# Two spectral filters mixed by a gate: rows folded four ways, the swapped spectrum made by DMA, products in column chunks

## The chip, the core and the metric

The kernel runs on one core of a Trainium2 chip. TensorE (PE) multiplies matrices into PSUM; ScalarE (ACT) and VectorE (DVE) read PSUM and write SBUF; GpSimd (POOL) takes small copies; transfers are issued by SyncE's queue (SP) and carried by 16 DMA engines. The metric is device time in microseconds (us), the median of the runs.

## The reference

`x` is a real image of 2048 rows and 1024 columns in bfloat16. Two filters A and B have complex weights of 2048 rows and 513 columns each, given as real and imaginary parts. Both filters read the same `x`; `B_x` is not used.

```python
def _A_ref(x, w_r, w_i):
    X = rfft2(x.astype(float32))
    X = X * (w_r + 1j * w_i)
    return irfft2(X, s=(S, D)).astype(bfloat16)

x = A_x
g = sigmoid((x * gate_w).sum(-1, keepdims=True))
a = _A_ref(x, A_w_r, A_w_i)
b = _B_ref(x, B_w_r, B_w_i)
return g * a + (1 - g) * b
```

## The kernel before

The transforms are matrix products. A row number is split as n = 64 n1 + n2 (n1 of 32, n2 of 64), a row frequency as k = k1 + 32 k2. The seven stages are numbered as in the code; a "t" is one of 16 values of the first row frequency, and each t yields two of the 32 values of k1.

- Load (L252 to L266). SP issues constants M in four pieces alternating with four pieces of 1 MB of x, then F2 and CK, then the weights W as 32 transfers of 64 partitions, 4 rows of 513 values each. Real parts lie on partitions 0 to 63, imaginary parts on 64 to 127.
- Stage 1 (L273 to L300). Partition p holds 16 whole rows of x. The column half is folded: DVE makes a reversed copy of the second half (L274), PE multiplies the plain and the reversed half with M (L295), ACT evicts (L299). Between the reversed copies DVE forms the 16 dot products of x with `gate_w` (L278).
- Stage 2 (`stage2`, L306). For one t: 8 matmuls of 512 columns (L314), one ACT eviction (L317), one tiny POOL copy into STAR (L319).
- Stage 4 (`stage4`, L322). For one t, four matmuls of 512 columns make the row spectrum X and four more make the swapped one (real and imaginary parts exchanged between partition halves, from shifted columns of the same matrices, `64 * sw`); L336, evicted by ACT at L339. Then four DVE products of 128x1024 with W (L348), two into R_A, two into R_W. Stage 2 of t+1 stands ahead of stage 4 of t on PE.
- After all products, in this order: the table U5 is loaded over F2 and M (L358); the gate's diagonal (L362), a matmul that spreads it (L366), the sigmoid (L371); the Nyquist column ("star", L376, L384, L386); a POOL copy (L393); a correction of column 0 (L410, L412).
- Stage 5 (L436 to L461): 32 groups g of 16 matmuls of 128 columns (L449), evicted by ACT and DVE in turn (L458). DVE forms the gated row tables (`rbgen`, L429), four small products for each r.
- DI is loaded after the last stage 5 matmul, over dead rows of R_A (L465).
- Stage 6 (`stage6`, L470) is 16 matmuls of 128 for one r with an ACT eviction (L485); stage 7 (`stage7`, L487) is 8 matmuls of 512 (L494), one ACT eviction (L498), two DVE additions (L502) and a store of 256 KB. Stage 6 of r+2 stands ahead of stage 7 of r.

The order on every engine is the order in which `P.add` is called; `Prog` turns the read and write keys into semaphore waits. A wait on DVE is for a count of its finished instructions, so whoever waits for one DVE result waits for all that stand ahead of it:

```python
                elif op.needed:
                    c += 1
                    op.sem, op.count = sem("s_" + e), c
```

Of the kernel before, what the change touches and what calls it, by code (L numbers as in the profile page):

```python
# [4 lines left out]
dt = mybir.dt  # L5
ACT = mybir.ActivationFunctionType
ALU = mybir.AluOpType
# [3 lines left out]
RW = 514  # L11
NROW = 64 * RW
# [9 lines left out]
def make_consts():  # L22

    C = {}
    pi2 = 2 * np.pi
    n1 = np.arange(32)
    M = np.zeros((32, 4, 16, 16, 2, 4))
    for b in range(4):  # L30
        for r in range(16):
            n2 = 16 * b + r
            for t in range(16):
                if t == 0:
                    M[:, b, r, 0, 0, b] = 1.0
                    M[:, b, r, 0, 1, b] = (-1.0) ** n1
                else:
                    ph = pi2 * t * (64 * n1 + n2) / 2048
                    M[:, b, r, t, 0, b] = np.cos(ph)
                    M[:, b, r, t, 1, b] = -np.sin(ph)  # L40
    M = M.reshape(128, 16, 1, 128)
    C["M"] = np.concatenate([M, -M], axis=2).reshape(128, 16 * 256)
    dd = np.arange(512)[:, None]
    ll = np.arange(512)[None, :]
    th = pi2 * ll * (dd + 0.5) / 1024
    cs, sn = np.cos(th), np.sin(th)
    sn[:, 0] = (-1.0) ** np.arange(512)
    F2 = np.stack([cs.reshape(4, 128, 512), sn.reshape(4, 128, 512)])
    C["F2"] = F2.transpose(2, 0, 1, 3).reshape(128, 8 * 512)
# [3 lines left out]
    def four(kind, pm):  # L53
# [11 lines left out]
        return Ac.reshape(128, 128), Bs.reshape(128, 128)  # L65

    blocks = []
    for kind in ("gen", "sp"):
        for pm in range(2):
            for m in four(kind, pm):  # L70
                blocks += [m, m[:, :64]]
# [3 lines left out]
    KIA = np.block([[c, s], [-c, -s]])  # L75
    KIB = np.block([[-s, c], [-s, c]])
    blocks += [KIA, KIB]
# [10 lines left out]
    blocks += [T1, T3, -T3, T3z, -T3z, T2, T4, -T4, T4z, -T4z]  # L88
    blocks += [np.eye(128), np.ones((128, 128))]
    C["CK"] = np.concatenate(blocks, axis=1)  # L90
    row = np.arange(128)
    l2, k1, f = row % 2, (row // 2) % 32, row // 64
# [11 lines left out]
    C["SM"] = SM  # L104
    DI = np.zeros((128, 2, 2, 2, 512))
    d = np.arange(512)[None, :]
    for lb in range(2):
        for h in range(2):
            l0 = 128 * lb + np.arange(128)
            l = l0 + 257 * h  # L110
            if h == 1 and lb == 1:
                l[127] = 256
            l = l[:, None]
            cl = np.where(l == 0, 1.0, 2.0) / D
            a = pi2 * l * (d + 0.5) / 1024
            DI[:, lb, h, 0] = cl * np.cos(a)
            DI[:, lb, h, 1] = -cl * np.sin(a)
# [81 lines left out]
def bass_gated_mix__spectral_gfnet__spectral_gfnet__prompt_kernel(nc, A_x, A_w_r, A_w_i, B_x, B_w_r, B_w_i, gate_w, out):  # L199
# [6 lines left out]
    NK = C["CK"].shape[1]  # L206
    R_A = sb("R_A", NROW)
    R_W = sb("R_W", NROW)
    R_F = sb("R_F", 16384)
    R_M = sb("R_M", 8192)  # L210
    CK = sb("CK", NK)
    RING = sb("RING", 7184)
    RB = sb("RB", 2048)
    DZ = sb("DZ", 2048)
# [4 lines left out]
    ZS = sb("ZS", 16, dt.float32)  # L219
    PS = nc.alloc_psum_tensor("PS", [128, 4096], dt.float32)  # L220

    def sl(t, off, dims, p0=0, np_=128):
        n = t.shape[1]
        return AP(t, p0 * n + off, [[n, np_]] + [list(x) for x in dims])
# [4 lines left out]
    CSO, XAO, XSO = 0, 3 * 1028, 3 * 1028 + 2048  # L229
    FB = {}  # L230
    i = 0
    for kind in range(2):
        for pm in range(2):
            for m in range(2):
                FB[kind, pm, m] = 192 * i
                i += 1
    KIAo, KIBo = 1536, 1664
    TO = [1792 + 128 * j for j in range(10)]
    IDo, ONo = 1792 + 1280, 1792 + 1408
# [4 lines left out]
    xv = x2.rearrange("(p r) d -> p r d", r=16)  # L244
    outv = out2.rearrange("(p r) d -> p r d", r=16)

# [3 lines left out]
    u16 = dt.uint16  # L250
    GWo = 0
    dma("act", sl(RB, GWo, [(1, 1024)]), AP(gate_w.tensor, gate_w.offset, [[0, 128], [1, 1024]]), w=["gw"])  # L252
    dma("act", SM[:], cst_sm.ap(), w=["SM"])
    for c in range(4):
        dma("sp", sl(R_M, c * 1024, [(1, 1024)]).bitcast(u16), cst["M"].ap()[:, c * 1024:(c + 1) * 1024], w=[("M", c)])
        dma("sp", sl(R_A, c * 4096, [(1024, 4), (1, 1024)]), xv[:, 4 * c:4 * c + 4, :], w=[("x", c)])
    dma("sp", sl(R_M, 4096, [(1, 4096)]).bitcast(u16), cst["F2"].ap(), w=["F2"])
    dma("sp", CK[:].bitcast(u16), cst["CK"].ap(), w=["CK"])
    for c in range(4):
        for hi in range(2):  # L260
            a = 4 * c if hi == 0 else 28 - 4 * c
            for f in range(2):
                for ri in range(2):
                    src = wsrc[f, ri].rearrange("(k2 k1) l -> k2 k1 l", k1=32)[:, a:a + 4, :]
                    dst = sl(R_W, (f * 32 + a) * RW, [(RW, 4), (1, 513)], p0=64 * ri, np_=64)
                    dma("sp", dst, src, w=[("W", a // 4, f, ri)])  # L266

    def bank(b):
        return ("ps", b)

    for c in range(4):  # L273
        P.add("dve", lambda e, c=c: e.tensor_copy(  # L274
            sl(RING, (c % 3) * 2048, [(512, 4), (1, 512)]), sl(R_A, 4 * c * 1024 + 1023, [(1024, 4), (-1, 512)])),
            r=[("x", c)], w=[("xr", c % 3)])
        for r in range(4 * c, 4 * c + 4):
            P.add("dve", lambda e, r=r: e.tensor_tensor_reduce(  # L278
                out=sl(RING, 6144, [(1, 1024)]), in0=sl(R_A, r * 1024, [(1, 1024)]), in1=sl(RB, GWo, [(1, 1024)]),
                scale=1.0, scalar=0.0, op0=ALU.mult, op1=ALU.add, accum_out=ZS[:, r:r + 1]),  # L280
                r=[("x", c), "gw"], w=["zjunk"], a=["z"])

        for j in range(4):
            u = (c * 4 + j) % 4
            for q in range(4):
                r = 4 * c + q
                for h in range(2):
                    if h == 0:
                        lh = sl(R_A, r * 1024 + 128 * j, [(1, 128)])
                        rh = sl(R_M, r * 256, [(0, 2), (1, 128)])  # L290
                    else:
                        lh = sl(RING, (c % 3) * 2048 + q * 512 + 128 * j, [(1, 128)])
                        rh = sl(R_M, r * 256, [(1, 256)])
                    o = ps(u * 1024 + q * 256, [(1, 256)])
                    P.add("pe", lambda e, o=o, lh=lh, rh=rh, h=h: e.matmul(o, lh, rh, start=(h == 0), stop=(h == 1)),  # L295
                          r=[("x", c), ("M", c), ("xr", c % 3)], w=[bank(2 * u + q // 2)])
            src = ps(u * 1024, [(128, 2), (1, 128), (256, 4)])
            dst = sl(R_F, j * 4096 + 4 * c, [(2048, 2), (16, 128), (1, 4)])
            P.add("act", lambda e, s=src, d=dst: e.activation(d, s, ACT.Copy),  # L299
                  r=[bank(2 * u), bank(2 * u + 1)], a=["F1"])  # L300


    order = list(range(1, 16)) + [0]
    ALLX = ["zjunk", ("xr", 0), ("xr", 1), ("xr", 2)]

    def stage2(i):  # L306
        t = order[i]
        b0 = 2 * (i % 2)
        for cs in range(2):
            for j in range(4):  # L310
                lh = sl(R_F, (j * 2 + cs) * 2048 + t * 128, [(1, 128)])
                rh = sl(R_M, 4096 + (cs * 4 + j) * 512, [(1, 512)])
                o = ps((b0 + cs) * 512, [(1, 512)])
                P.add("pe", lambda e, o=o, lh=lh, rh=rh, j=j: e.matmul(o, lh, rh, start=(j == 0), stop=(j == 3)),  # L314
                      r=["F1", "F2"], w=[bank(b0 + cs)])
        ro = CSO + (i % 3) * 1028
        P.add("act", lambda e: e.activation(sl(RING, ro, [(513, 2), (1, 512)]), ps(b0 * 512, [(512, 2), (1, 512)]), ACT.Copy),  # L317
              r=[bank(b0), bank(b0 + 1)], w=[("CS", i % 3)] + ALLX)
        P.add("pool", lambda e: e.tensor_copy(STAR[:, t:t + 1], sl(RING, ro + 513, [(1, 1)])),  # L319
              r=[("CS", i % 3)], a=["STAR"])  # L320

    def stage4(i):  # L322
        t = order[i]
        kind = 0 if t else 1
        ro = CSO + (i % 3) * 1028
        k1s = (t, 32 - t) if t else (0, 16)
        for sw in range(2):
            b0 = 4 + 2 * sw
            for pm in range(2):
                for m in range(2):  # L330
                    lh = sl(CK, FB[kind, pm, m] + 64 * sw, [(1, 128)])
                    if m == 0:
                        rh, o = sl(RING, ro, [(1, 512)]), ps((b0 + pm) * 512, [(1, 512)])
                    else:
                        rh, o = sl(RING, ro + 514, [(1, 511)]), ps((b0 + pm) * 512 + 1, [(1, 511)])
# [16 lines left out]
    for i in range(16):  # L352
        if i + 1 < 16:
            stage2(i + 1)
        stage4(i)
# [222 lines left out]
```

## Time and profile before

| | us |
|---|---|
| median of 3 runs | 181.21 (181.05 to 181.98) |
| span of the profiled execution | 179.5 |
| PE busy / weight load busy | 150.9 / 99.0 |
| DVE busy | 120.5 |
| ACT busy | 112.9 |
| POOL busy | 11.5 |
| bytes moved by DMA | 23.35 MB |

The profiled execution's own time is its span; the runs are timed without the profile, and the difference between 181.21 and 179.5 lies around the span. Busy shares are averages over stages with different limits, so the prediction goes by windows of the span and by the chain of work that ended last. A matmul counted as busy may be waiting inside a full pipeline. Line numbers are those of the kernel before.

### The profile page before, as it was taken

Reading aid. Unit: us, or ns where it says so; the run is one execution under the profiler, and the core shown is the slowest. Engines: PE = TensorE matmul, PEld = TensorE weight load, DVE = VectorE, ACT = ScalarE, POOL = GpSimd, SP = SyncE. Lnnn points to the kernel's source line nnn. Section 1 sums busy time; section 2 is a strip of 40 time slices with the busy share of each in tenths; the row PEclk is TensorE's granted clock in tenths of the full one; section 3 lists DMA queues with packets and bytes.
Section 4 is the critical chain, followed back from the end, with each engine's and each line's share of the span. In section 5 each row is a group of like instructions: output and inputs, shape, how many; then the busy total and the mean of one; then the engine's idle time right before and its main releaser. Section 6 shows DMA issues by size and latency. Waiting matters only on the chain.

```text
span 179.5 us, 3207 instructions
## 1 busy us (share of the span) xinstructions
PE 150.9 (84%) x1304; PEld 99.0 (55%) x1304; DVE 120.5 (67%) x233; ACT 112.9 (63%) x120; POOL 11.5 (6%) x22
## 2 busy tenths in 40 slices
PE   0099557999999999998424999999978999999991
PEld 0078445444444444443102999999966666656640
DVE  0199997067877777787974277888852787765463
ACT  2049668588898888888626355466555665565550
POOL 0000000011131131122001000000000000000000
PEclk9999999999999999999975599999999999999999
DMA  5999999999999940003800000000041213322323
GB/s 131 357 417 430 355 194 193 195 192 198 194 195 198 194 93 0 4 0 84 383 0 0 0 4 4 0 4 0 4 164 75 112 63 119 118 79 100 117 111 123
DMA packets 13038, 23.35 MB, mean 130 GB/s; under 512 B 1121, under 2 KB 9313, under 8 KB 12129
## 3 DMA queue, kind: packets, MB, share of 16 engines
q1 hardware_dynamic: 12736, 22.89, 48.4%
q10 hardware_dynamic: 288, 0.26, 0.6%
q8 instruction: 10, 0.16, 0.4%
q14 instruction: 4, 0.02, 0.1%
HBM read 18.96 MB, written 4.19 MB: 129 GB/s over the span
## 4 chain that ended last, share of the span: by engine, by line
PE 71%; DVE 13%; DMA 7%; ACT 5%; issue 2%; DVEq 0%; SPq 0%; ACTq 0%
PE PS L449 18%; PE PS L314 15%; PE PS L494 15%; PE PS L336 13%; DVE RING L278 7%; PE PS L481 6%; DMA R_A<-in_A_x_dram 4%; DMA R_A<-c_DI 3%; ACT R_F L299 2%; DVE DZ L362 1%; DVE RING L274 1%; DVE R_W L348 1%; ACT RING L339 1%; PE PS L366 1%; DVE R_A L348 1%
## 5 line engine op out<-in xcount | busy, mean ns | idle before, releaser
L339 ACT ACTIVATE RING<-PS 128x1024 bf16<-128x1024 f32 x32 | 32.8, 1024 | 3.5
L449 PE MATMUL PS<-CK,R_A 128*128 128x128 bf16 x256 | 32.6, 230 | 0.0
L449 PE MATMUL PS<-CK,R_W 128*128 128x128 bf16 x256 | 32.6, 230 | 0.0
L449 PEld LDWEIGHTS PS<-CK,R_W 128*128 128x128 bf16 x256 | 31.7, 145 | 0.0
L449 PEld LDWEIGHTS PS<-CK,R_A 128*128 128x128 bf16 x256 | 31.6, 145 | 0.0
L314 PE MATMUL PS<-R_M,R_F 128*128 128x512 bf16 x128 | 30.1, 379 | 1.2 <-ACT R_F L299 1.2
L336 PE MATMUL PS<-RING,CK 128*128 128x512 bf16 (+1 forms) x128 | 30.5, 379 | 0.6 <-ACT RING L339 0.5
L502 DVE TENSOR_TENSOR R_A<-R_A,PS 128x512 bf16<-128x512 f32 x32 | 20.6, 683 | 15.4 <-ACT R_A L498 10.2
L494 PE MATMUL PS<-R_A 128*128 128x512 bf16 x128 | 29.9, 379 | 0.5 <-DMA R_A<-c_DI 0.5
L348 DVE TENSOR_TENSOR R_A<-RING,R_W 128x1024 bf16<-128x1024 bf16 x32 | 22.0, 689 | 12.0 <-ACT RING L339 12.0
L295 PE MATMUL PS<-R_M,R_A 128*128 128x256 bf16 x64 | 16.3, 297 | 12.8 <-DVE RING L274 12.8
L485 ACT ACTIVATE R_A<-PS 128x1024 bf16<-128x1024 f32 x16 | 16.3, 1024 | 16.7 <-PE PS L481 16.7
L348 DVE TENSOR_TENSOR R_W<-RING,R_W 128x1024 bf16<-128x1024 bf16 x32 | 22.0, 689 | 6.6 <-ACT RING L339 6.6
L299 ACT ACTIVATE R_F<-PS 128x1024 bf16<-128x1024 f32 x16 | 15.2, 1032 | 12.6 <-PE PS L295 12.6
L314 PEld LDWEIGHTS PS<-R_M,R_F 128*128 128x128 bf16 x128 | 12.4, 98 | 16.4 <-ACT R_F L299 1.5
L336 PEld LDWEIGHTS PS<-RING,CK 128*128 128x128 bf16 x128 | 12.4, 98 | 16.3 <-ACT RING L339 1.6
L278 DVE CUSTOM_DVE_ANT_0 RING<-R_A,RB 128x1024 bf16<-128x1024 bf16 x16 | 19.6, 1223 | 0.4
L317 ACT ACTIVATE RING<-PS 128x1024 bf16<-128x1024 f32 x16 | 16.4, 1028 | 4.9 <-PE PS L314 4.3
L494 PEld LDWEIGHTS PS<-R_A 128*128 128x128 bf16 x128 | 11.9, 98 | 12.5 <-DMA R_A<-c_DI 0.7
L295 PE MATMUL PS<-R_M,RING 128*128 128x256 bf16 x64 | 16.2, 297 | 0.0
L319 POOL COPY STAR<-RING 128x1 bf16<-128x1 bf16 x16 | 10.6, 662 | 73.6 <-ACT RING L317 73.6
L295 PEld LDWEIGHTS PS<-R_M,R_A 128*128 128x128 bf16 x64 | 6.8, 107 | 14.6 <-DMA R_A<-in_A_x_dram 9.0
(48 smaller groups left out, 141.1 us busy)
## 6 DMA issues: line engine op xcount, KB each, us to landing
R_A<-in_A_x_dram SPq DMA_DIRECT2D x4, 1024.0 KB, 10.4
out_dram<-R_A SPq DMA_DIRECT2D x16, 256.0 KB, 2.0
R_W<-in_A_w_r_dram SPq DMA_DIRECT2D x8, 256.5 KB, 12.9
R_W<-in_A_w_i_dram SPq DMA_DIRECT2D x8, 256.5 KB, 13.0
R_W<-in_B_w_r_dram SPq DMA_DIRECT2D x8, 256.5 KB, 13.1
R_W<-in_B_w_i_dram SPq DMA_DIRECT2D x8, 256.5 KB, 13.4
R_M<-c_U SPq DMA_DIRECT2D x1, 2048.0 KB, 7.5
R_M<-c_M SPq DMA_DIRECT2D x4, 256.0 KB, 8.5
```

Of the source, the lines that this page charges most:

```text
L278: P.add("dve", lambda e, r=r: e.tensor_tensor_reduce(out=sl(RING, 6144, [(1, 1024)]), in0=sl(R_A, r * 1024, [(1, 1024)]), in1=sl(RB, GWo, ...
L295: P.add("pe", lambda e, o=o, lh=lh, rh=rh, h=h: e.matmul(o, lh, rh, start=(h == 0), stop=(h == 1)), r=[("x", c), ("M", c), ("xr", c % 3)], ...
L299: P.add("act", lambda e, s=src, d=dst: e.activation(d, s, ACT.Copy), r=[bank(2 * u), bank(2 * u + 1)], a=["F1"])
L314: P.add("pe", lambda e, o=o, lh=lh, rh=rh, j=j: e.matmul(o, lh, rh, start=(j == 0), stop=(j == 3)), r=["F1", "F2"], w=[bank(b0 + cs)])
L317: P.add("act", lambda e: e.activation(sl(RING, ro, [(513, 2), (1, 512)]), ps(b0 * 512, [(512, 2), (1, 512)]), ACT.Copy), r=[bank(b0), bank ...
L336: P.add("pe", lambda e, o=o, lh=lh, rh=rh, m=m: e.matmul(o, lh, rh, start=(m == 0), stop=(m == 1)), r=["CK", ("CS", i % 3)], w=[bank(b0 + ...
L339: P.add("act", lambda e, xo=xo, b0=b0: e.activation(sl(RING, xo, [(1, 1024)]), ps(b0 * 512, [(1, 1024)]), ACT.Copy), r=[bank(b0), bank(b0 ...
L348: P.add("dve", lambda e, d=dst, a=xin, b=win: e.tensor_tensor(out=d, in0=a, in1=b, op=ALU.mult), r=[("X", sw, i % 2)] + wk, a=[("prod", sw ...
L449: P.add("pe", lambda e, o=o, t=t, l0=l0, ab=ab: e.matmul(o, sl(t, l0, [(257, 128)]), sl(CK, KIAo if ab == 0 else KIBo, [(1, 128)]), start= ...
L485: P.add("act", lambda e, s=src, d=dst: e.activation(d, s, ACT.Copy), r=[bank(b0), bank(b0 + 1)], w=[("Y", r)], after=[last5])
L494: P.add("pe", lambda e, o=o, lh=lh, rh=rh, q=q: e.matmul(o, lh, rh, start=(q == 0), stop=(q == 3)), r=[("Y", r), "DI"], w=[bank(b0 + ri)])
L502: P.add("dve", lambda e, od=od, h=h: e.tensor_tensor(out=od, in0=es, in1=ps((b0 + 1) * 512, [(1, 512)]), op=ALU.add if h == 0 else ALU.sub ...
```

## The change

The whole forward part is laid out anew.

- x is folded four ways: partition 2p+h holds half h of 32 rows. It arrives as 16 transfers of 64 alternate partitions with rows of 512 values (1 KB). M arrives in pieces of 128 values (256 bytes) in eight transfers; POOL makes the negated half of M. There are 32 dot products of 512, some of them now among stage 2.
- Stage 2 has matmuls of 256 columns, 32 for a pair of t, and one ACT eviction of 128x2048 for both; stage 4 has 8 matmuls of 512 for the pair, no swapped ones, and one ACT eviction of 128x2048 into XF. There are 8 pairs.
- Real and imaginary parts lie on even and odd partitions (`PERM`). The swapped spectrum is made by four SBUF-to-SBUF transfers for each pair, each of 64 alternate partitions and two rows of 512 values.
- W goes to alternate partitions too. Three of its eight groups are issued before the first swap, the other five each behind the swaps of a pair.
- Products are made for groups of 16 values of k1 rows (`prod_lb0`, columns 0 to 127 of each half row) during stage 4, and for the other columns afterwards in chunks (`prod_lb1`, `prod_last`). A product reads all rows of a chunk at once, up to 128x2048.
- The gate's diagonal is one DVE instruction at pair 4. Star stands ahead of the seventh group of stage 5, column 0 ahead of the eleventh, the POOL copy ahead of the twenty-first. DVE evicts only every second group from the twenty-first on. The row tables are made by four gate products of 128x2048 and eight scalings.
- U5 has its own tile and is loaded behind the swaps; DI is loaded into XF once all readers of the spectrum are done. Stages 6 and 7 keep their matmuls.

In the new kernel all matmuls of the stages carry the line of the helper `mm`, evictions and copies that of `move`, products that of `mul`. The core of the diff:

```diff
+PERM = np.array([64 * (p % 2) + p // 2 for p in range(128)])
...
-    for c in range(4):
-        dma("sp", sl(R_M, c * 1024, [(1, 1024)]).bitcast(u16), cst["M"].ap()[:, c * 1024:(c + 1) * 1024], w=[("M", c)])
-        dma("sp", sl(R_A, c * 4096, [(1024, 4), (1, 1024)]), xv[:, 4 * c:4 * c + 4, :], w=[("x", c)])
...
-                    dst = sl(R_W, (f * 32 + a) * RW, [(RW, 4), (1, 513)], p0=64 * ri, np_=64)
...
+    for c in range(8):
+        dma("sp", sl(RP, S_S1 + c * 1024, [(256, 4), (1, 128)]).bitcast(u16),
+            cst["M"].ap()[:, c * 512:(c + 1) * 512].rearrange("p (r n) -> p r n", n=128), w=[("M", c)])
+        for h in range(2):
+            dma("sp", sl(RP, S_A0 + c * 2048, [(512, 4), (1, 512)], p0=h, np_=64, step=2),
+                AP(xt, xoff + c * 4096 + h * 512, [[32768, 64], [1024, 4], [1, 512]]), w=[("x", c, h)])
...
+                dst = sl(RP, (S_S0 if f == 0 else S_A1) + row * RW, [(RW, n), (1, 513)], p0=ri, np_=64, step=2)
...
+        move("act", sl(XF, ta * RW, [((30 - 2 * ta) * RW, 2), (RW, 2), (1, 512)]), ps(2048, [(1024, 2), (512, 2), (1, 512)]), r=banks(4, 4), w=[("X", i)], after=P.rd["F1"])
+        for pm in range(2):
+            row = 30 - ta if pm else ta
+            for pa in range(2):
+                src = sl(XF, row * RW, [(RW, 2), (1, 512)], p0=1 - pa, np_=64, step=2)
+                dst = sl(RP, S_S1 + row * RW, [(RW, 2), (1, 512)], p0=pa, np_=64, step=2)
+                dma("sp", dst, src, r=[("X", i)], w=[("XS", i, pm, pa)], after=[s1])
...
+        first = [mul(sl(RP, S_A0 + o, rows), sl(XF, o, rows), sl(RP, S_S0 + o, rows), r=deps + ["z"], a=[("PA", key)], after=[s1])
+                 for o, rows, deps in todo]
+        second = [mul(sl(RP, S_S0 + o, [(SLOT, 2)] + rows), sl(RP, S_S1 + o, [(0, 2)] + rows), sl(RP, S_S0 + o, [(-SLOT, 2)] + rows),
+                      r=deps, a=[("PS", key)], after=[op]) for (o, rows, deps), op in zip(todo, first)]
+        for (o, rows, deps), op in zip(todo, second):
+            mul(sl(RP, S_A1 + o, rows), sl(XF, o, rows), sl(RP, S_A1 + o, rows), r=deps, a=[("PA", key)], after=[op])
+
+    def prod_lb0(g):
+        prods([(4 * g, 4, [(g, 0)]), (28 - 4 * g, 4, [(g, 1)])], 0, 128, 0)
+
+    def prod_lb1(q, s):
+        c0, cn = ((128, 56), (184, 64))[q]
+        prods([(8 * s, 8, [(2 * s, 0), (2 * s + 1, 0)]), (24 - 8 * s, 8, [(2 * s, 1), (2 * s + 1, 1)])], c0, cn, 1 + q)
...
+        if i in (0, 2, 4):
+            load_group(i // 2 + 1, 0)
+        if i in (1, 3, 5):
+            load_group((i + 1) // 2, 1)
+        stage4(i)
...
+        if i % 2:
+            prod_lb0(i // 2)
...
+    for q in range(2):
+        for s in range(2):
+            prod_lb1(q, s)
+    prod_last()
...
+    def star():
...
+        move("dve", XST[:, 0:32], ps(0, [(1, 32)]), r=[bank(0)], w=["XST0"])
+        mm(ps(32, [(1, 32)]), sl(CK, SWo, [(1, 128)]), XST[:, 0:32], True, True, ["CK", "XST0"], [bank(0)])
+        move("dve", XST[:, 32:64], ps(32, [(1, 32)]), r=[bank(0)], w=["XST1"])
...
     for n, g in enumerate(gorder):
+        if n == 6:
+            star()
+        if n == 10:
+            column0()
+        if n == 20:
+            copies()
         u = (n + 2) % 4
+        ck = 0 if g < 16 else 1 if g < 23 else 2 if g < 31 else 3
...
+        eng = "act" if n < 20 or n % 2 == 0 else "dve"
+        move(eng, dst, ps(u * 1024, [(1, 128), (128, 8)]), r=banks(2 * u, 2), a=[("L4", g // 16)])
+        if n in (22, 24, 26, 28):
+            gated((n - 22) // 2)
+        if n in (26, 30):
+            rbgen((n - 26) // 4)
...
+    dma("sp", sl(XF, DIo, [(1, 4096)]).bitcast(u16), cst["DI"].ap(), w=["DI"], after=xdead)
```

## The prediction

> **What bounds the kernel now.** I read the page's head first, then the windows table, the chain, the groups. Times are us of one profiled execution (span 179.5); the median of the runs is 181.2, so 1.7 lies around the span and I add it at the end.
>
> ```profile
> PE 150.9 (84%) x1304; PEld 99.0 (55%) x1304; DVE 120.5 (67%) x233; ACT 112.9 (63%) x120; POOL 11.5 (6%) x22
> PEclk9999999999999999999975599999999999999999
> DMA  5999999999999940003800000000041213322323
> GB/s 131 357 417 430 355 194 193 195 192 198 194 195 198 194 93 0 4 0 84 383 0 0 0 4 4 0 4 0 4 164 75 112 63 119 118 79 100 117 111 123
> DMA packets 13038, 23.35 MB, mean 130 GB/s; under 512 B 1121, under 2 KB 9313, under 8 KB 12129
> ```
>
> PE is busy 84%, yet the DMA engines are full for the first 65 us, first at 420 GB/s (x, in 8 KB runs), then at 194 (the weights W, 32 transfers of 256 rows of 1026 bytes). The windows (length; busy of PE, PEld, DVE, ACT, POOL; clock; DMA share; GB/s) separate the two:
>
> ```profile
> 10.00:20.00 10.00, 8.42 (x61) 6.58 (x59) 9.79 (x19) 7.65 (x8) 0.00 (x0) 1.00 1.02 422
> 40.00:50.00 10.00, 10.00 (x48) 4.54 (x47) 7.77 (x12) 8.86 (x9) 2.14 (x3) 1.00 1.13 194
> 100.00:110.00 10.00, 10.00 (x151) 10.00 (x150) 6.28 (x12) 5.03 (x5) 0.00 (x0) 0.88 0.01 2
> 110.00:120.00 10.00, 10.00 (x169) 10.00 (x168) 7.95 (x15) 5.65 (x6) 0.00 (x0) 1.00 0.01 3
> 150.00:160.00 10.00, 10.00 (x96) 6.46 (x95) 7.88 (x24) 5.56 (x9) 0.00 (x0) 1.00 0.29 107
> ```
>
> Between 40 and 50 PE and DMA are both full: PE sets the end there and W stays hidden. The chain (start, length, what) says the same:
>
> ```profile
> 74.09 1.73 PE PS L314 x8
> 75.81 1.73 PE PS L336 x8
> ...
> 89.80 0.60 DVE R_W L348
> 90.40 2.62 DVE DZ L362 x16
> ...
> 98.64 32.57 PE PS L449 x512
> 131.21 0.02 issue
> 131.23 4.90 DMA R_A<-c_DI
> 136.13 0.05 issue
> 136.17 1.90 PE PS L494 x8
> ```
>
> So: load and stage 1 to 30.7, stages 2 and 4 on PE to 82.7, drain and gate to 98.6, stage 5 to 131.2, a wait for DI, stages 6 and 7. Two group rows give sizes for ACT and DVE:
>
> ```profile
> L339 ACT ACTIVATE RING<-PS 128x1024 bf16<-128x1024 f32 x32 | 32.8, 1024 | 3.5
> L429 DVE TENSOR_TENSOR RB<-R_M,RING 128x256 bf16<-128x256 bf16 x24 | 5.4, 284 | 1.1 <-PE PS L481 1.1
> ```
>
> **Stages 2 and 4.** PE loses half its columns: stage 2 has 128 matmuls of 256 instead of 512 columns, stage 4 has 64 of 512 instead of 128. At 1.73 per eight matmuls of 512 that is 27.6 of 55.3 saved. ACT now evicts 16 tiles of 2048: from 592 ns (512) and 1024 ns (1024) the slope gives 1.89 each. Each stage has one set of four banks, so PE fills one while ACT empties the other: ACT sets 3.9 per pair of t, against 6.9 of PE before. Started at 27, the first stage 4 result is evicted at 37, the last at 64. This saving is not on the path if the products wait for something else, and they do.
>
> **The price of DMA runs.** The stores of 2 KB runs move 107 GB/s at share 0.29, so 369 at full share, 89 ns per run and engine; x's 8 KB runs at 414 (422/1.02) take 316. A line through both: 13 ns plus 37 ps per byte, so 51 ns for 1 KB and 23 for 256 bytes. W's 1026 bytes cost 16 x 1026 / 194 = 85 ns, 1.7 times the line. Either the length and odd alignment cost this, or its 64 adjoining partitions.
>
> **Load.** x goes from 8 KB to 4096 runs of 1 KB on alternate partitions, M from 2 KB to 4096 runs of 256 bytes. By the line x is 4096 x 51/16 = 13.1 and M 5.8. Bounds: 9.9 (422 GB/s) and 21.7 (W's price) for x; 2.5 and 21.7 for M. I take the line, which lies between neighbours of the same form. The before load starts moving at about 4 (1.57 MB landed at 8.2), so 22.9, and F2 with CK (1.26 MB at 422) takes it to 26. SP's issue (0.34 to 0.88 each before its queue filled, 24 of them, some 15) is below that. Dots, reversals and POOL's eight negations of M lie beside it (POOL is 6% busy); DVE needs 2.5 per chunk against 2.4 of DMA, so stage 1 still ends near 27.
>
> The Trainium skill, DMA: Bandwidth & Descriptors, Specifications, says that runs under 512 bytes are read, changed and written back; this speaks against M's new layout, no row here shows it, and at twice the line the sum would be an estimated 5.8 us longer.
>
> **W and the swap.** W is the same 8.4 MB in the same rows, only on every second partition: 43.2 at 194 GB/s (high end), 26.1 by the line (low end). The nearest row is W's own, so I keep 43.2. New are 32 SBUF-to-SBUF transfers of 128 KB, 4096 runs of 1 KB: 13.1 by the line, 9.9 at bytes, 21.7 at W's price; rows of 1024 bytes are aligned, so I take 13.1. They sit in SP's queue between W groups: each waits for its stage 4 eviction, and behind it waits the next W group. While W is three groups ahead the engines never run dry. The last swap lands 2 after its issue (the stores' row): T = 26 + 43.2 + 13.1 + 2 = 84.3, against 64 on ACT. DMA has become the bound.
>
> The Trainium skill, SBUF — State Buffer, Door 1: The DMA port swizzle, says that partitions 0 to 63 reach only 8 of 16 ports and gives 196 GB/s for such a transfer; W's 194 here agrees with it. By that page alternate partitions reach all 16, and W would take an estimated 26 us instead of 43.
>
> **After T.** DVE multiplies in chunks. A 128x1024 product takes 0.60 in the chain; with the slope from 284 ns (256) to 689 (1024) a 2048 takes 1.14, an 896 0.53, a 1792 1.00. All later products queue behind the last first-chunk group, which needs the last swap: 4.7 + 2 x 4.1 + 2 x 4.7 + 1.9 = 24.2. Stage 5 starts after 4.7 and runs six groups. Then PE meets star's swap matmul, which reads XST, and XST's copy stands on DVE behind all products: PE waits some 13 there with 26 groups behind it. Star itself is 0.9 (four hops of the 0.2 cast and matmul rows). Groups 6 to 19: 14 x 0.96 (169 matmuls per 10), 1.7 for a lower clock after the pause (151 instead of 169 matmuls at clock 0.88 cost 1.1 after 7 of pause; here the pause is longer), column0 1.1 and 1.4 for its two ACT moves (0.47 each) in front of bank 0: 17.6. Groups 20 to 31: DVE carries six evictions of 1.2 (L458's row), four gates of 1.13 and four row-table instructions of 0.75 (L416: 784 ns), 14.7 after a first wait of 1.9: 16.6 against 11.4 of PE. Then stage 6(0) 0.9, its eviction 1.07, 6(2) 0.9: 2.9. From the first stage 7 matmul to the end is unchanged: 179.5 - 136.17 = 43.3. Sum: 24.2 + 0.9 + 17.6 + 16.6 + 2.9 + 43.3 = 105.5. Gone are DZ (2.62), the DI wait (4.9, now under stage 5; 4.9 again if the swapped rows' readers ended later) and U5's late load.
>
> **Sum.** 84.3 + 105.5 = 189.8 span, plus 1.7: 191.5; I say 191. No change would need T = 74.
>
> **Rivals.** A, faster: alternate partitions spread W over more paths and W falls to the line. DMA then ends at 26 + 26.1 + 13.1 + 2 = 67.2; the issue on SP (0.6 to 0.7 for a transfer, eight per iteration) and ACT's 64 plus the last swap make it 69: 176. It decides once W and swaps together take under 46 instead of 56.3. For it: the line leaves 34 of W's 85 ns unexplained by run length. Against: SP's queue shows W transfers accepted every 1.2 to 1.3 throughout, though they alternate between the lower and upper 64 partitions, so two transfers in flight on different halves brought nothing.
> C, much slower: the half-partition form itself costs, so x and swaps too pay 85 ns: 4 + 21.7 + 5.8 + 3 + 43.2 + 21.7 + 2 = 101.4, 208.6. For it: every W transfer is 64 partitions wide, and so are all of these. Against: only W's rows are off a 4-byte multiple.
> D, part relief: W at about 65 ns (33), T near 75 to 78: 182 to 185.
> That the PE halving shows in full needs T = 64 + 3, which is A.
>
> **How the numbers follow.** Mine 0.42, A 0.30, C 0.16, D 0.12. The range 174 to 204 leaves out most of C and the low edge of A; mine alone spans 184 (swaps at bytes, a shorter stall) to 199 (M doubled, swaps dearer). A measurement can tell about 0.5% (0.9 us) from no change. Faster: A and a little of D, 0.32; same 0.04; slower 0.64.
>
> **What would show it.** Right: W near 194 GB/s in the windows, the last swap landing at 80 to 88, PE and ACT idle before it, PE waiting over 10 in stage 5 on DVE's XST copy, a DVE-paced end of stage 5. Wrong: windows after 26 above 300 GB/s with swaps following ACT closely (A); x landing after 30 (C); PE not waiting at star, which would take 13 off.

## The result and the profile after

The changed kernel takes 196.4 us (median of 4 runs, 194.8 to 199.1) against 181.2 before: ratio 1.079, interval 1.074 to 1.085. Some executions ran in a slower state of the chip (199.1 here, and further on 199.8 of the control, 183.3 and 184.7 of the run with stage 1 on ACT, 183.6 of the run with star early), and the ratios leave them out. The profiled execution has a span of 195.0, and its own time is 196.8, so 1.8 lies around the span. A second set of four runs, taken as a control (below), gave 197.4. The forecast was 191, slower, within 174 to 204.

The page's head after, engines, slices, clock and DMA:

```profile
PE 136.3 (70%) x1230; PEld 99.5 (51%) x1241; DVE 111.0 (57%) x192; ACT 96.4 (49%) x91; POOL 16.2 (8%) x22
...
PE   0653854939999985300790069999946999999991
...
PEclk9999688696999997555588557999996999999999
DMA  5999996000179999979100041000000022232223
GB/s 145 281 320 312 393 350 210 0 2 0 54 196 296 287 298 279 279 255 363 71 2 0 0 170 49 0 3 5 0 3 0 20 91 108 108 111 108 102 81 143
```

PE, ACT and DVE do less than before, PE by 14.6 us, and the kernel is slower: the time went into pauses. DMA is no longer full from 0 to 65; it is idle from 34 to 49 and near full again from 54 to 92, the last of it U5's load, and the clock row dips where PE has paused. The chain (start, length, what) shows three stretches. In these views L262 is `mm`, L266 and L267 are `move` on ACT and on DVE, L270 is `mul`, L315 a dot product and L253 a transfer; RP holds x, W and the products, XF the spectrum, U the reversed copies. First stage 1:

```profile
20.06 4.37 PE PS L262 x23
24.42 0.02 issue
24.45 1.22 DVE XF L267
25.67 0.60 DVE GW L315
...
27.01 0.35 DVE U L267
27.36 0.05 issue
27.41 3.24 PE PS L262 x15
30.65 0.02 issue
30.67 1.23 DVE XF L267
```

PE's matmuls, then DVE's eviction (XF), two dot products (GW), the reversed copy (U) of the next chunk, then PE again. DVE and PE wait for each other in turn, a ring: stage 1 ends at 39.9, though the last x was issued at 16.6. The waits (waiting engine and line, for whom; total, times, longest) show both sides of it:

```profile
DVE XF L267 <- PE PS L262: 12.4, 5, 3.3
PE PS L262 <- DVE U L267: 10.7, 4, 3.4
```

Second, the swaps, whose last issue on SP ends at 86.5 (queue of SP: start, length, transfer):

```profile
67.66 2.62 SPq L253 DMA_DIRECT2D RP<-XF  x4
70.33 0.62 SPq L253 DMA_DIRECT2D RP<-in_A_w_r_dram  x1
71.01 0.64 SPq L253 DMA_DIRECT2D RP<-in_A_w_i_dram  x1
71.69 0.62 SPq L253 DMA_DIRECT2D RP<-in_B_w_r_dram  x1
72.34 0.62 SPq L253 DMA_DIRECT2D RP<-in_B_w_i_dram  x1
73.00 2.96 SPq L253 DMA_DIRECT2D RP<-XF  x4
```

Eight issues take 5.3 without a gap, for each of the first five pairs of t, behind whose swaps a group of W stands. Third, what follows the swaps:

```profile
88.91 24.30 DVE RP L270 x42
113.22 0.11 DVE XST L267
...
113.87 6.62 PE PS L262 x64
```

and in the waits PE's pause at star:

```profile
PE PS L262 <- DVE XST L267: 11.5, 2, 11.2
```

### The profile page after: what moved, and what is told of

Its sections match the earlier page's. It is cut to its first block, busy times and chain, and to the rows that moved or that the text cites. A ratio compares the mean times of both kernels' runs of the same rounds, so it can differ in the third digit from the quotient of the medians.

```text
span 195.0 us, 3078 instructions
## 1 busy us (share of the span) xinstructions
PE 136.3 (70%) x1230; PEld 99.5 (51%) x1241; DVE 111.0 (57%) x192; ACT 96.4 (49%) x91; POOL 16.2 (8%) x22
## 4 chain that ended last, share of the span: by engine, by line
PE 52%; DVE 26%; ACT 10%; DMA 4%; issue 4%; SPq 1%; DVEq 1%
PE PS L262 52%; DVE RP L270 14%; ACT XF L266 8%; DVE RP L267 3%; DVE XF L267 3%; DMA RP<-in_A_x_dram 2%; DVE U L270 2%; DMA RP<-XF 2%; SPq L253 1%; DVE RP L452 1%; DVE GW L315 1%; DVE U L267 1%; ACT CG L266 1%; ACT RP L266 1%; DVE XF L565 0%
## 5 line engine op out<-in xcount | busy, mean ns | idle before, releaser
L266 ACT ACTIVATE XF<-PS 128x1024 bf16<-128x1024 f32 (+2 forms) x51 | 50.6, 1022 | 53.1 <-PE PS L262 50.8
L262 PE MATMUL PS<-CK,RP 128*128 128x128 bf16 x512 | 37.0, 243 | 13.4 <-DVE RP L270 12.0
L262 PE MATMUL PS<-RP 128*128 128x128 bf16 (+1 forms) x320 | 38.8, 252 | 9.7 <-DMA RP<-in_A_x_dram 6.3
L262 PEld LDWEIGHTS PS<-CK,RP 128*128 128x128 bf16 x512 | 36.3, 149 | 14.6 <-DVE RP L270 12.9
L266 ACT ACTIVATE RP<-PS 128x1024 bf16<-128x1024 f32 (+1 forms) x28 | 26.6, 989 | 32.9 <-PE PS L262 32.8
L565 DVE TENSOR_TENSOR XF<-XF,PS 128x512 bf16<-128x512 f32 x32 | 20.6, 684 | 21.6 <-PE PS L262 21.5
L262 PEld LDWEIGHTS PS<-RP 128*128 128x128 bf16 x320 | 24.6, 107 | 15.2 <-DMA RP<-in_A_x_dram 6.3
L270 DVE TENSOR_TENSOR RP<-XF,RP 128x1024 bf16<-128x1024 bf16 (+2 forms) x40 | 20.8, 580 | 18.7 <-PE PS L262 8.5
L262 PE MATMUL PS<-XF 128*128 128x512 bf16 x121 | 29.2, 379 | 0.4
L262 PE MATMUL PS<-RP,U 128*128 128x256 bf16 x64 | 20.7, 347 | 10.8 <-DVE U L267 10.7
L315 DVE CUSTOM_DVE_ANT_0 GW<-RP,GW 128x512 bf16<-128x512 bf16 x32 | 22.6, 706 | 0.9
L270 DVE TENSOR_TENSOR RP<-RP 128x2048 bf16<-128x2048 bf16 (+2 forms) x20 | 19.2, 1007 | 0.0
L262 PE MATMUL PS<-CG,CK 128*128 128x511 bf16 (+1 forms) x60 | 16.2, 407 | 3.4 <-ACT XF L266 2.9
L262 PE MATMUL PS<-FZ,XF 128*128 128x256 bf16 x128 | 16.3, 283 | 3.1 <-ACT CG L266 2.0
L267 DVE CAST RP<-PS 128x1024 bf16<-128x1024 f32 x6 | 7.3, 1221 | 19.3 <-PE PS L262 19.3
L262 PEld LDWEIGHTS PS<-XF 128*128 128x128 bf16 x128 | 11.9, 98 | 11.8
L266 ACT ACTIVATE CG<-PS 128x2048 bf16<-128x2048 f32 x8 | 15.0, 1876 | 5.0 <-PE PS L262 5.0
L262 PEld LDWEIGHTS PS<-FZ,XF 128*128 128x128 bf16 x128 | 12.3, 100 | 7.4 <-ACT CG L266 4.1
L262 PEld LDWEIGHTS PS<-RP,U 128*128 128x128 bf16 x64 | 7.9, 123 | 14.6 <-DVE U L267 12.4
L267 DVE CAST XF<-PS 128x1024 bf16<-128x1024 f32 x5 | 6.1, 1225 | 12.4 <-PE PS L262 12.4
L262 PEld LDWEIGHTS PS<-CG,CK 128*128 128x128 bf16 x64 | 6.0, 103 | 11.9 <-ACT XF L266 5.2
```

Source lines behind the costliest of these rows:

```text
L262: return P.add("pe", lambda e: e.matmul(o, lh, rh, start=start, stop=stop), r=r, w=w)
L266: return P.add("act", lambda e: e.activation(d, s, ACT.Copy), **kw)
L267: return P.add(eng, lambda e: e.tensor_copy(d, s), **kw)
L270: return P.add("dve", lambda e: e.tensor_tensor(out=d, in0=i0, in1=i1, op=ALU.mult), **kw)
L315: P.add("dve", lambda e: e.tensor_tensor_reduce(out=sl(GW, 512, [(1, 512)]), in0=sl(RP, S_A0 + r * 512, [(1, 512)]), in1=sl(GW, 0, [(1, 51 ...
L565: P.add("dve", lambda e, od=od, h=h: e.tensor_tensor(out=od, in0=es, in1=ps((b0 + 1) * 512, [(1, 512)]), op=ALU.add if h == 0 else ALU.sub ...
```

## The experiments

All edits but the first are to the changed kernel; the control, which has no edit, stands seventh. They ran on two chips, on which the kernel before took 181.35 and 181.81. Since the first stage 2 matmul of the changed kernel falls anywhere from 35.8 to 40.0 with no edit near it, gains are read between landmarks of one trace of each kernel and not from the time alone.

**W on alternate partitions, in the kernel before**

```diff
-                    dst = sl(R_W, (f * 32 + a) * RW, [(RW, 4), (1, 513)], p0=64 * ri, np_=64)
+                    dst = sl(R_W, (f * 32 + a) * RW, [(RW, 4), (1, 513)], p0=ri, np_=64, step=2)
```

> The kernel before, with W's real and imaginary rows put on even and odd partitions; the products then pair the wrong rows, so the output is not the reference's, and only W's transfers are read. Theory P (the 64 adjoining partitions made W dear): W moves at 350 to 400 GB/s and its last transfer lands near 46 instead of 67; the time stays within 1 us of before, because PE sets the end there. Rival L (the odd 1026-byte length made it dear): W stays at 194 GB/s and ends at 67.

Windows of this run (length; PE, PEld, DVE, ACT, POOL; clock; DMA share; GB/s):

```profile
30.00:40.00 10.00, 9.27 (x43) 4.22 (x44) 3.11 (x6) 6.83 (x7) 1.07 (x3) 1.00 1.10 349
40.00:50.00 10.00, 10.00 (x48) 4.51 (x47) 7.77 (x12) 8.84 (x9) 2.11 (x3) 1.00 0.62 197
50.00:60.00 10.00, 10.00 (x48) 4.57 (x47) 7.41 (x12) 8.85 (x10) 1.83 (x4) 1.00 0.00 1
```

The same 8.4 MB in the same 1026-byte rows move at 349 GB/s instead of 194 and are done near 46. That is 16 x 1026 / 349 = 47 ns a run, even under the line's 51. So it was the 64 adjoining partitions, not the length. The time of the one run is 180.7 against 181.35: W was hidden, as the profile before said. (The edit also gives `sl` its argument `step`.)

**W back on partition halves, in the changed kernel**

```diff
-                dst = sl(RP, (S_S0 if f == 0 else S_A1) + row * RW, [(RW, n), (1, 513)], p0=ri, np_=64, step=2)
+                dst = sl(RP, (S_S0 if f == 0 else S_A1) + row * RW, [(RW, n), (1, 513)], p0=64 * ri, np_=64)
```

> The changed kernel with W's real rows on partitions 0 to 63 and imaginary rows on 64 to 127 as in the kernel before; products then pair the wrong rows and the output is not the reference's. If 64 adjoining partitions make W dear here too: W back at about 85 ns a run, a pair of swaps and W 6.9 instead of 5.3, the last swap 3 to 6 us later, and the time with it. If SP's issue alone sets the pace: within 1 us of the changed kernel.

```profile
60.00:70.00 10.00, 7.93 (x51) 4.45 (x49) 4.86 (x6) 9.51 (x6) 1.02 (x3) 1.00 1.13 205
...
94.21 24.30 DVE RP L270 x42
```

The same window of the profile after, and the same products in the control:

```profile
60.00:70.00 10.00, 9.62 (x65) 5.92 (x65) 4.77 (x6) 9.41 (x6) 0.58 (x3) 1.00 0.98 288
...
88.30 24.30 DVE RP L270 x42
```

203.6 us against the control's 197.4. W and swaps together move 205 GB/s at full share, where the changed kernel has 288. SP's last swap issue ends at 86.7, as in the control (86.0), but the last products start at 94.2 instead of 88.3: 5.9 later. The first swap was issued 3.1 earlier than in the control (47.0 for 50.2), which is not the edit's, so between these landmarks the edit costs 9.0. This is the case that the forecast took as the likeliest, and it is worth 6 to 9, not the 17 (43.2 less 26.1) that it charged.

**Stage 1 evicted by ACT alone**

```diff
-            move("dve" if k % 3 == 2 else "act", dst, src, r=banks(2 * u, 2), a=["F1"])
+            move("act", dst, src, r=banks(2 * u, 2), a=["F1"])
```

> The changed kernel with all 16 evictions of stage 1 on ACT instead of every third on DVE. Theory R (DVE's evictions close a ring: the reversed copy of a chunk waits behind an eviction that waits for PE, and PE waits for that copy): stage 1 ends near 27 instead of 40, the swaps move with it, the time falls by 10 to 13 us to 184 to 186. Rival K (PE is slow by its lower clock or M arrives late): stage 1 still ends after 36 and the time falls by less than 4.

181.8 us (8 runs), ratio to the kernel before 0.9975, interval 0.992 to 1.003: the one line gives back all that the change had lost, and the time is 2 below the range expected. Its chain at the end of stage 1:

```profile
22.40 0.95 PE PS L262 x7
23.36 0.02 issue
23.38 1.95 ACT XF L266 x2
...
25.37 1.94 PE PS L262 x16
```

The first stage 2 matmul is at 25.4 instead of 40.0 in the profile after and 39.0 in the control, and PE waits 1.1 for the reversed copies where it waited 10.7; the ring is shown. The edit also takes five evictions, 6.1 us, off DVE, but the amount of work was not what held stage 1: DVE stood idle for 12.4 there, waiting for PE, and without that stage 1 would have ended near an estimated 27.5 (39.9 less 12.4). The clock is 1.00 up to 60, where the profile after had 0.71 to 0.83 between 20 and 50, so a part of the 14 is the clock that the ring's pauses cost. How ring, work and clock divide was not tried.

**Star ahead of the last products**

```diff
-        if n == 6:
-            star()
...
+        if i == 7:
+            star()
         if i % 2:
             prod_lb0(i // 2)
```

> The changed kernel with star (matmuls, XST copies, PST) issued after the last stage 4 and ahead of the last first-chunk products. Theory Q (PE's 11 us wait in stage 5 is DVE's queue ahead of XST): the wait is gone and the time falls by 8 to 12 us; what is late next is the chunk products that stage 5 reads at its 17th group, so some 2 us may come back. Rival: PE would have had to wait for the products anyway, and the time falls by less than 4.

180.0 us (the other run 183.6). DVE's first gate product in stage 5, here and, below, in the control:

```profile
117.80 1.22 DVE U L270
...
133.72 1.21 DVE U L270
```

It comes 15.9 earlier. The products of the third group start 2.7 earlier (81.5 for 84.2), which the edit does not explain. So 13.2 is the edit's, more than the 8 to 12 expected: the wait of 11.6 that the control has at star, and 1.6 more, perhaps by the clock. PE still waits for XST, but between stage 4 and the last products, where it has nothing to do.

**All of W issued first**

```diff
+    for g in range(4):
+        load_group(g, 0)
+        load_group(g, 1)
...
-        if i in (0, 2, 4):
-            load_group(i // 2 + 1, 0)
-        if i in (1, 3, 5):
-            load_group((i + 1) // 2, 1)
```

> The changed kernel with all eight W groups issued ahead of the first swap. Theory S (eight issues of 0.65 on SP per pair, 5.3, set the swaps' pace, not ACT's 3.9): swaps follow ACT's eviction, the last lands near 84 instead of 88.5, the time falls by 4 to 5 us. Rival M (the DMA engines set it by bytes or runs): W then stands ahead of the swaps and the last lands no earlier; the time moves by under 1.

186.3 us (2 runs). SP's queue now has all swaps in one row, and in the control the first and the last of them in these two:

```profile
46.45 29.70 SPq L253 DMA_DIRECT2D RP<-XF  x32
...
50.17 2.58 SPq L253 DMA_DIRECT2D RP<-XF  x4
78.23 7.80 SPq L253 DMA_DIRECT2D RP<-XF  x12
```

From the first swap to the end of the last takes 29.7 against 35.9 in the control (50.2 to 86.0): 6.2 gained, for 4 to 5 expected, by ACT's pace of 3.9 in place of SP's 5.3. The swaps start 3.7 earlier as well, which is not the edit's. The DMA engines are at share 0.36 to 0.58 from 50 on, so neither bytes nor runs set the pace in this run. But the edit takes W out of the swaps' stretch and so relieves the engines as well as SP, and in the changed kernel they were near full there (share 0.98 and 1.00 from 60 to 80). For SP speak three rows. With W and swaps together the engines can do more than the 288 GB/s of that stretch: 352 at share 1.09 between 40 and 50 in the run with all four edits. SP's issues keep their 0.62 to 0.66 there, where in the run with W on halves, at share 1.13, some take 1.2 to 2.0. And in the run with stage 1 on ACT the chain goes from 46.5 to 64.6 through SP's issues alone:

```profile
46.54 0.38 SPq L253
...
63.96 0.64 SPq L253
64.60 0.04 issue
64.64 3.87 DMA RP<-XF
```

**Stage 5 evicted by ACT alone**

```diff
-        eng = "act" if n < 20 or n % 2 == 0 else "dve"
+        eng = "act"
```

> The changed kernel with all 32 evictions of stage 5 on ACT. Theory T (six evictions, four gate products and four table scalings in turn on DVE set the end of stage 5): the end of stage 5 comes 3 to 5 us earlier and so does the time. Rival (ACT at 0.95 to 1.0 a group is no faster, or the tables are needed at that time anyway): under 1.5.

190.0 us (2 runs) against 197.4. The last evictions of stage 5 in the chain, here and, below, in the control:

```profile
119.96 21.52 ACT RP L266 x22
...
145.51 1.14 DVE RP L267
```

Products start 2.4 earlier (81.8 for 84.2), not by the edit; the span is 7.3 shorter, so 4.9 came after. Of these 2.8 stand at the end of stage 5 (141.5 for 146.7, less the 2.4): DVE's queue did set it, and ACT's chain there runs 22 evictions in 21.5, 0.98 each. The other 2.1 come behind it: in the control PE pauses for 3.4 there and has a clock of 0.50 from 146 to 152, in this run it pauses for 0.7 and keeps 1.00.

**The changed kernel again**

> The changed kernel itself, as a control on this chip. If the 2 to 5 us by which the earlier experiments were ahead before their first swap were chance of PE's granted clock, its times spread over 192 to 198 and the clock between 20 and 50 differs from profile to profile; if they were due to the edits, it repeats 195 to 197 with clock 0.7 to 0.8 there.

197.4 us (195.7 to 199.8), span 195.3. The clock was 0.83, 1.00 and 0.83 in the three windows from 20 to 50, where the first profile had 0.71, 0.78 and 0.83. Neither case came whole: the total repeats, but the place of the lost clock does not. That the few us upstream in the other runs are of that kind is likely and not shown: the two profiles without an edit have the first swap at 51.2 and 50.2, the four with an edit behind stage 1 at 46.5 to 47.7.

**All four edits**

> The changed kernel with the four edits together: stage 1 evicted by ACT, star early, W up front, stage 5 evicted by ACT. If the four causes are independent and on one path: stage 1 ends near 26, the last swap lands near 65, stage 5 runs from 71 to 104, the span is 151 to 156 and the time 153 to 158, faster than both kernels. If DVE's products (24 after the last swap) or the clock after the pause take over, 160 to 168.

159.0 us (158.8 to 160.1), ratio to the kernel before 0.877, interval 0.872 to 0.881: faster than both kernels. The page's head and SP's swaps:

```profile
PE 127.5 (81%) x1241; PEld 92.6 (59%) x1241; DVE 99.6 (63%) x181; ACT 105.7 (67%) x102; POOL 20.4 (13%) x22
```
```profile
43.75 22.39 SPq L253 DMA_DIRECT2D RP<-XF  x32
```

Its window in which W and swaps move together:

```profile
40.00:50.00 10.00, 9.36 (x63) 5.63 (x62) 0.00 (x0) 9.51 (x6) 0.56 (x3) 1.00 1.09 352
```

It is 1 above the range expected of independent causes. Stage 1 is early now, but W's 36 issues hold SP until 43.7, 9 after the first swap could have gone (34.9 in the run with ACT evictions alone), and then 32 swaps of 0.70 each end at 66.1. Stage 5 starts at 74.8, not 71, and with all evictions on ACT takes 35.7, not 33. The order that issues W only as far as the swaps leave room was not tried.

## Why the prediction was right, and where only its sum was

The direction and the range held, and what stands behind T came close for the reasons given. T itself, 84.3 for some 88.9, was near by luck: W was charged 19 too much, stage 1 13 too little, and the DMA engines, which the forecast made the bound, did not set it. Of the signs named, PE's wait at star and the DVE-paced end of stage 5 came; W near 194 GB/s did not (370, 288 and 281 in the windows from 20, 60 and 70).

- Stages 2 and 4: right. ACT sets 3.9 per pair (1.94 of PE and 1.89 of ACT in turn), and most of the saving is off the path: the last result is evicted at 79.05, the last swap issued by 86.5.
- The line for DMA runs: right. 51 ns for 1 KB was 47 for W's rows on alternate partitions, and x and M, 5.2 MB, had moved by about 20 (215 and 319 GB/s in the first two windows) for 22.9. So M's runs of 256 bytes did not cost twice the line, which would have taken them to an estimated 28.7.
- Stage 1 "still ends near 27": wrong by 13. The step counted DVE's 2.5 per chunk as work beside PE. It is in PE's ring: the eviction waits for PE, the next reversed copy stands behind it, PE waits for the copy. The sum of busy time fitted (39.9 less DVE's waits of 12.4 is 27.5); the order in DVE's queue was not walked through. With the evictions on ACT it was 25.4.
- W keeps its price, 43.2: wrong; the low end, 26.1, was the truth (24.1 at 349 GB/s). Two explanations of 34 ns were named, and the one nearest by row was taken. The Trainium skill, SBUF — State Buffer, Door 1: The DMA port swizzle, says that DMA bandwidth depends on how many of the 16 ports the partitions reach, and gives 8 for partitions 0 to 63. Both runs on W agree: 194 GB/s on adjoining partitions (205 with the swaps among it), 349 on alternate ones. The argument held against rival A, that transfers on the two halves in turn brought nothing, is still true of the kernel before (194); it says nothing of transfers on alternate partitions.
- That the DMA engines never run dry while W is three groups ahead: wrong. They stood still from 34 to 49, because the five other groups of W stand in SP's queue behind the first swap, and that waited for its stage 4 result until 51.2.
- The swaps' pace: the price of 13.1 for their runs did not matter. SP's 0.65 for each issue, named under rival A only, times eight is 5.3 for each of the first five pairs and set the pace.
- T: 84.3 forecast; the products after the last swap start at 88.9. Too much for W, too little for stage 1 and for SP.
- After T: 105.5 forecast, 195.0 - 88.9 = 106.1 measured. The products took 24.3 for 24.2; PE's wait at star 11.2 for some 13; groups 6 to 19 from 113.9 to 133.6, 19.7 for 17.6; DVE's end of stage 5 from 133.6 to 147.7, 14.1 for 16.6; the rest 47.3 for 46.2.

Rival A had the mechanism of DMA right and 176 for it. The kernel that takes the ring out of stage 1 and nothing else ran 181.8, so even there A was 6 too fast. Rival C is out: no 64-partition transfer on alternate partitions paid 85 ns. Rival D, a partial relief (65 ns a run), is out as well: the run was 47 ns.

## What to carry to other kernels

Adding busy time engine by engine tells what could fit, not when it runs: walk each in-order queue through one turn and look for an instruction that waits for another engine while something that engine needs stands behind it. Here two such places (a PSUM eviction ahead of the next chunk's copy, 42 products ahead of a tiny copy) cost some 14 (the clock among it) and 13 us, and moving them took a few lines. When many small transfers leave one queue, multiply the issue time by their number before asking what the bytes cost.

## What the runs showed of the hardware

- Transfers to 64 partitions, one behind the other, moved 349 GB/s on every second partition and 194 on 64 adjoining ones, with the same rows.
- SP took about 0.65 us for each transfer of 128 or 256 runs, 0.62 of it in the issue, and no less with the DMA engines far from full (2.58 for the first four swaps of the control, at share 0.65 between 50 and 60).
- PE's granted clock fell to 0.50 in windows where it hardly worked (80 to 90 after), and to between 0.71 and 0.83 in stage 1, where it merely paused for 2.0 to 3.4 us in each turn (in the profile after); in the run with the ring gone it stayed at 1.00 there.
